# Deltanet and soft-MoE on one core: POOL's two-input work moved to VectorE and ScalarE, one form of inverse for all groups, a new order of work

## The chip, the cores and the metric

One core of a Trainium2 chip. The time is device microseconds of one execution, median of several runs. Engines: PE (TensorE), DVE (VectorE), ACT (ScalarE), POOL (GpSimd), SP (SyncE, here only a DMA queue).

## What is computed

A delta-rule attention scan over 768 steps for 4 batches x 8 heads of dimension 48, then a soft mixture of experts over its output. All is float32.

```python
k_n = k / (norm(k) + 1e-6)
for t in range(S):                       # S = 768
    y[t] = q[t] @ state
    v_old = state.T @ k_n[t]
    state += beta[t] * outer(k_n[t], v[t] - v_old)
x = y.transpose(...).reshape(3072, 384)
logits = x @ phi                         # 32 slots
d = softmax(logits, axis=0); slot_input = d.T @ x
slot_out[e] = relu(slot_input[e] @ w1[e]) @ w2[e]     # 8 experts, F = 1024
out = softmax(logits, axis=1) @ slot_out
```

## The kernel before, in words

The scan is cut into 24 chunks of 32 steps, and four chunks make a group (6 groups). For a chunk, all 32 (batch, head) pairs are worked on together.

*Preparation of a chunk* (`prep`, lines 472 to 561). K and Q are loaded padded (line 457), transposed by PE (543) and copied from PSUM (327 on ACT or 329 on DVE, a helper `copy`). PE forms the products K K^T and Q K^T (495). From them come L, in two masked ACT copies (507) whose halves are added (523, POOL or DVE), and A, copied in two halves and then masked on POOL (533, "mkA").

*Inverse of a group* (`invert`, 577 to 795). A DVE transpose brings the 32x32 matrices of 4 chunks x 32 pairs to one per partition (584, "spread"). Norms of k come from its diagonal (594 to 619; Newton steps on DVE for group 0, on POOL for the others). Then a forward elimination of 31 columns, each a product (648) and a subtraction (659) on DVE, each waiting for the one before. Line 663 transposes back, and `pairs` (566) writes two masked halves TP per chunk, on ACT (572) or POOL (574). Group 0 has another form: two 16-column eliminations side by side (704, 720), whose corner comes from small PE products (772, 785) and masks on POOL or ACT (758, 760).

*Scan of a chunk* (`chunk`, 802 to 889). V is scaled by the norms on POOL (813). PE reads the state (824), DVE subtracts (834), PE solves with TP (843), the result is copied, PE updates the state (860), whose four PSUM banks are copied in two parts of 64x768. A gives the output (876). Four DMAs a chunk re-lay it for the next stage (887, on SP's or ACT's queue).

*Routing of a group* (`route`, 895): transposes (903), logits (915), running column softmax, slot sums (971), row softmax (1000). *Experts*: weights are loaded by 56 DMAs (1026, 1034, on SP's queue) into the memory of scan buffers as these die; two layers (1119, 1150); outputs (1179, 1186 on ACT, 1188 on DVE) through 6 buffers, stored from SP and POOL (1192).

*The order.* Every operation is declared with the engines that could run it and a cost. `Plan.run` then simulates the engines ahead of the build: at each step it takes, for each engine, the ready operation of highest priority (length of the path behind it, plus a bias) among those that can start within 0.15 us of the first, and picks the engine whose choice starts first. The program is emitted in that order; on the chip each engine and queue works through its own list in order, waiting on semaphores.

Of the kernel before, what the change touches and what calls it, by code (L numbers as in the profile page):

```python
# [15 lines left out]
LAT = {"PE": 0.22, "DVE": 0.10, "ACT": 0.12, "POOL": 0.15, "SP": 0.05, "DMA": 1.9}  # L16
# [19 lines left out]
class Plan:  # L36
    def __init__(self, slots, banks, fixed, window):
        self.ops, self.slots, self.banks, self.window = [], slots, banks, window
        self.fixed, self.order, self.bias, self.limits = fixed, {}, 0.0, {}

# [3 lines left out]
    def op(self, name, engines, fn, reads=(), writes=(), bias=0.0, dma=0.0,  # L44
           uses=(), after=()):
        o = Op(name, engines, fn, list(reads), list(writes), bias + self.bias, dma)
# [57 lines left out]
    def run(self, backing=()):  # L104
# [23 lines left out]
        ready = [o for o in self.ops if not wait[o]]  # L128
# [21 lines left out]
        def place(v):  # L150
            if v.kind != "ps":
                if v.tag not in slots:
                    return 0.0, ()
                if self.order[v.tag][heads[v.tag]] is not v or not tags[v.tag]:
                    return None
                s = min(tags[v.tag])
                return s[0], s
            best = None
            n = v.banks
            if used.get(v.tag, 0) + n > self.limits.get(v.tag, 99):  # L160
                return None
            for i in range(0, self.banks - n + 1 if n < 4 else 1):
                if not any(held[i:i + n]):
                    t = max(bank[i:i + n])
                    if best is None or (t, -i) < (best[0], -best[1]):
                        best = (t, i)
            return best

        while left:
            pick = None  # L170
            for e in free:
                cands = []
                for o in ready:
                    for x, cost in o.engines:
                        if x != e:
                            continue
                        t = max([free[e]] + [seen(d, e) for d in o.deps])
                        ok = True
                        for v in o.writes:
                            if v.where is None:  # L180
                                p = place(v)
                                if p is None:
                                    ok = False
                                    break
                                t = max(t, p[0])
                            else:
                                t = max(t, v.avail)
                        if ok:
                            cands.append((t, o, cost))
                if not cands:  # L190
                    continue
                t0 = min(c[0] for c in cands)
                t, o, cost = max((c for c in cands if c[0] <= t0 + self.window),
                                 key=lambda c: (c[1].prio, -c[0]))
# [4 lines left out]
            for v in o.writes:  # L199
                if v.where is None:  # L200
                    p = place(v)
# [32 lines left out]
            for x in o.outs:  # L234
                wait[x] -= 1
                if not wait[x]:
                    ready.append(x)
# [6 lines left out]
def kernel(  # L244
# [11 lines left out]
    nc = tc.nc  # L256
# [9 lines left out]
    HC = C // 2  # L266
# [10 lines left out]
                lb=1056, tt=C * C, pr=256, Dt=512, Dc=512, M1=512, D0=1024,  # L277
                P1=512, TP=U * 2 * C, R=U * D, U=U * D, Y=U * D, S=4 * B * G * D, X=B * Dm,
                XT=B * P, lT=P, dT=P, d=P, el=P, cT=P, wt=NKT * F, hr=F, hT=NFC * P, ob=Dm,
                sj=Dm, so=Dm, cw=P, sl=NKT * NSL)  # L280
    SLOTS = dict(K=11, Q=4, V=5, KQ=10, AT=10, Lc=2, Lx=2, lb=2, tt=2, pr=2, Dt=1, Dc=1,
                 M1=1, D0=1, P1=1, TP=8, R=2, U=2, Y=3, S=2, X=2, XT=3, lT=2, dT=1, d=1, el=1,
                 cT=NG, hr=1, hT=2, ob=6, sj=1, so=1, cw=2, sl=1)
    ALIAS = {("X", 1): [("D0", 0), ("Dt", 0)], ("XT", 0): [("Dc", 0)], ("XT", 1): [("M1", 0)],
             ("XT", 2): [("P1", 0)]}
    KEEP = ("cT",)
    OBP, HTP, RBIAS, EB, IBIAS, FETCH = 0, 11, 40.0, 60.0, -5.0, 0.0125
    TAIL = ("hr", "hT", "ob", "sj", "so", "cw", "sl")
    plan = Plan(SLOTS, 8, 0, 0.15)
    plan.limits = dict(tp=2, pg=2, py=2)  # L290
# [49 lines left out]
    def vc(n):  # L340
        return 0.06 + 0.00104 * n
# [9 lines left out]
    half = const("half", [P, 2])  # L351
    par = const("par", [P, 2])
    tri2 = const("tri2", [P, 2, C])
# [36 lines left out]
    def constants2(e):  # L390
        nc.vector.tensor_tensor(bdm, bdm, hm.unsqueeze(2).broadcast_to([P, 4, C]), op=ALU.mult)
        nc.vector.tensor_reduce(tri, bdm.rearrange("p h t -> p t h"), axis=AX.X, op=ALU.add)
        nc.vector.tensor_reduce(half, ident.rearrange("p (h a t) -> p a h t", h=4, a=2),
                                axis=AX.XY, op=ALU.add)
        nc.vector.tensor_reduce(par, ident.rearrange("p (h a t) -> p a h t", h=2, a=2),
                                axis=AX.XY, op=ALU.add)
        nc.vector.tensor_tensor(tri2, tri.unsqueeze(1).broadcast_to([P, 2, C]),
                                par.unsqueeze(2).broadcast_to([P, 2, C]), op=ALU.mult)
    op("const2", [("DVE", 1.4)], constants2, [cv], [cv])

    padv, s0v, d0v = {}, [val("", "st") for _ in range(SLOTS["S"])], val("", "st")
# [11 lines left out]
    for i in range(SLOTS["S"]):  # L413
        op(f"s0{i}", [("POOL", 1.5), ("DVE", 1.5)], lambda e, i=i: clear(e, where["S", i]), [],
           [s0v[i]])
    op("d0", [("POOL", 0.6)],
       lambda e: clear(e, where["D0", 0].rearrange("p (u s) -> p u s", s=C)[:, :, HC:C]), [], [d0v])

# [22 lines left out]
    op("bbx", [("PE", 0.7)], spread_b, [btv, selv], [pbb])  # L441
# [20 lines left out]
    def loads(cc):  # L462
        for src, d, t in ((k, Kv, "K"), (q, Qv, "Q"), (v, Vv, "V")):
            x = d[cc] = val(t, par=True)
            for h in range(4):
                op(f"ld{t}{cc}", [("SP", 0.45)] + ([("ACT", 0.42)] if cc < 4 else []),
# [5 lines left out]
    def prep(cc):  # L472
# [37 lines left out]
        def ev_a(x, np_):  # L510
            def fn(e):
                for g in range(G):
                    copy(e, sb(at, G, B, 2, C)[:, g], view(x, np_, np_ - 1)[:, g])
            return fn

        def evs_l(x, np_):
# [8 lines left out]
            op(f"adL{cc}", [("POOL", 0.62), ("DVE", 0.35)], add, [lx, lcp[cc]], [lc, lcp[cc]])  # L525

        def evs_a(x, np_):
            op(f"evA{cc}", pcost2(512), ev_a(x, np_), [x], [at], bias=EB)

            def mask(e):  # L530
                v_ = nc.vector if e == "DVE" else PO
                t = sb(at, U, 2, C)
                v_.tensor_tensor(t, t, tri2.unsqueeze(1).broadcast_to([P, U, 2, C]), op=ALU.mult)  # L533
            op(f"mkA{cc}", [("POOL", 1.15)], mask, [at, cv], [at])

        for a, src, L in ((0, Kv, "K"), (1, Qv, "Q")):
            s = src[cc]
# [6 lines left out]
            op(f"tr{L}{cc}", [("PE", 0.46)], tr,  # L544
# [5 lines left out]
            if split:  # L550
                x = val("pg", "ps", 2)
                op(f"gram{L}{cc}", pe(16, 0.45), gram((a,), x), [kq], [x] + ([at] if a else [lc, lx]))
# [4 lines left out]
        if not split:  # L557
            x = val("pg", "ps", 2)
            op(f"gram{cc}", pe(16, 0.87), gram((0, 1), x), [kq], [x, lc, lx, at])
            evs_l(x, 2)  # L560
            evs_a(x, 2)


    TPv, nTv, TTp = {}, {}, {}

    def pairs(n, c, src, reads, uses):
        x = TPv[GC * n + c] = val("TP", par=True)
        for i in range(2):
            def fn(e, i=i):
# [3 lines left out]
                else:  # L573
                    PO.tensor_scalar(dst, src(), par[:, i:i + 1], None, op0=ALU.mult)
            op(f"TP{GC * n + c}", [("ACT", 0.42), ("POOL", 0.9)], fn, reads + [cv], [x], uses=uses)

    def invert(n):
        lc = Lcv[n]
        lb, tt = val("lb", par=n == 0), val("tt")
# [6 lines left out]
        op(f"spread{n}", [("DVE", 1.6)], spread, [lc], [lb])  # L586
# [14 lines left out]
        def newton(e):  # L601
            v_ = nc.vector if e == "DVE" else PO
            for _ in range(3):
                v_.tensor_tensor(gm, nr, dg(), op=ALU.mult)
# [5 lines left out]
        op(f"nw{n}", [(E0, 2.6 if n == 0 else 4.5)], newton, [lb, s1], [s1])  # L610
# [5 lines left out]
        op(f"gm{n}", [("DVE", 0.5)], inv, [s1, bbv], [gv])  # L616
# [5 lines left out]
        if n:  # L622
            lm = lambda: sb(lb)[:, 0:C * C].rearrange("p (i j) -> p i j", j=C)

            def zero(e):
                PO.memset(sb(tt), 0.0)
            op(f"ttz{n}", [("POOL", 1.0)], zero, [], [tt])

            def diag(e):
                PO.tensor_copy(sb(tt)[:, 0:C * C:C + 1], gm)  # L630
            op(f"ttd{n}", [("POOL", 0.4)], diag, [gv], [tt])

            def scale(e):
                (nc.vector if e == "DVE" else PO).tensor_tensor(
                    lm(), lm(),
                    gm.unsqueeze(2).broadcast_to([P, C, C]), op=ALU.mult)
            op(f"lbs{n}", [("DVE", 1.15), ("POOL", 1.95)], scale, [lb, gv], [lb])
            for j in range(C - 1):
                m, w = j + 1, C - 1 - j
                pr = val("pr")  # L640

                def e1(e, j=j, m=m, w=w, pr=pr):
                    t, s, o = sb(tt, C, C), lm(), sb(pr)[:, 0:w * m]
                    if m == 1:
                        nc.vector.tensor_tensor(o, t[:, 0, 0:1].broadcast_to([P, w]), s[:, 1:C, 0],
                                                op=ALU.mult)
                    else:
                        nc.vector.tensor_tensor(  # L648
                            o.rearrange("p (i k) -> p i k", i=w),
                            t[:, j, 0:m].unsqueeze(1).broadcast_to([P, w, m]),  # L650
                            s[:, j + 1:C, j].unsqueeze(2).broadcast_to([P, w, m]), op=ALU.mult)
                op(f"el{n}.{j}a", [("DVE", vc(w * m))], e1, [tt, lb], [pr])

                def e2(e, j=j, m=m, w=w, pr=pr):
                    t, o = sb(tt, C, C), sb(pr)[:, 0:w * m]
                    d = t[:, 1:C, 0] if m == 1 else t[:, j + 1:C, 0:m]
                    if m > 1:
                        o = o.rearrange("p (i k) -> p i k", i=w)
# [638 lines left out]
```

## Time and profile before

| | us |
|---|---|
| median of 3 runs (lowest, highest) | 410.18 (409.32, 416.75) |
| profiled execution | 405.77 |
| its span in the profile | 404.1 |
| DVE copies, line 329: 512 / 768 / 384 / 256 elements | 0.686 x31 / 0.955 x21 / 0.554 x20 / 0.415 x10 |
| ACT copies, line 327, same sizes | 0.598 x39 / 0.806 x25 / 0.492 x28 / 0.389 x38 |
| POOL lines 533 / 813 / 523 / 574, mean | 1.335 x24 / 0.875 x24 / 0.751 x21 / 1.183 x9 |
| line 584 transpose / 663 transpose / 634 scaling | 1.965 / 1.245 / 1.224 |
| weight loads, 512 and 384 KB, issue to landing | 6.6 and 6.2 |

Rows of the profile read "line engine operation, output<-input, shape, count | busy us in total, mean ns of one | idle time before, and who ended it". In a timeline a row gives start, duration, engine, line, and in brackets the idle time before it with its releaser. SPq and ACTq are DMA issues on those queues. Issues don't count as an engine's busy time, but take time in its order.

### The profile page before, as it was taken

What the parts mean: (1) busy time and instruction counts of PE and PEld (TensorE: products, weight loads), DVE (VectorE), ACT (ScalarE), POOL (GpSimd) and SP (SyncE); (2) the same over time, 40 slices, a digit from 0 to 9 for tenths busy, and PEclk for the clock granted to TensorE, in tenths of its full rate; (3) what the DMA queues carried; (4) which work ended last, traced back from release to release, by engine and by line L of the source; (5) the groups of instructions that cost most, each with busy time, mean ns of one, the idle gap of its engine ahead of it and who ended that gap; (6) DMA issues with size and microseconds to landing.
All of it is one profiled execution on the core that took longest, in us unless ns stands there. A gap on an engine that the chain in (4) does not pass through costs nothing. (4 is left out here: it accounts for less than half of the span.)

```text
span 404.1 us, 14058 instructions
## 1 busy us (share of the span) xinstructions
PE 280.0 (69%) x5940; PEld 216.9 (54%) x5940; DVE 277.7 (69%) x633; ACT 131.7 (33%) x277; POOL 119.5 (30%) x198
## 2 busy tenths in 40 slices
PE   4775747879467875787648686567769663679872
PEld 3664537768346763676547465455657452333330
DVE  5179877958759899799899769787995531332143
ACT  0552353314442423445244053162237110100032
POOL 7166436313551134645064004350012000000033
PEclk9687575869869988699957579958998968669985
DMA  7646450345414454243211325743319977798057
GB/s 131 109 88 103 84 91 13 58 75 87 80 27 81 71 89 70 36 77 57 41 19 24 68 54 140 259 135 80 59 29 360 367 247 210 243 384 319 1 210 259
DMA packets 115151, 49.84 MB, mean 123 GB/s; under 512 B 105760, under 2 KB 107296, under 8 KB 115088
## 3 DMA queue, kind: packets, MB, share of 16 engines
q1 hardware_dynamic: 90352, 42.20, 40.2%
q10 hardware_dynamic: 23936, 4.33, 6.0%
q0 software_dynamic: 800, 2.41, 1.7%
q8 instruction: 47, 0.77, 0.8%
q14 instruction: 16, 0.13, 0.1%
HBM read 39.47 MB, written 4.72 MB: 109 GB/s over the span
## 5 line engine op out<-in xcount | busy, mean ns | idle before, releaser
L327 ACT ACTIVATE arena<-banks 128x512 f32<-128x512 f32 (+4 forms) x139 | 71.1, 536 | 149.4 <-PE banks L876 36.3
L329 DVE COPY arena<-banks 128x512 f32<-128x512 f32 (+4 forms) x89 | 57.6, 658 | 58.5 <-PE banks L903 18.5
L659 DVE TENSOR_TENSOR arena<-arena 128x31 f32<-128x31 f32 (+15 forms) x155 | 61.7, 398 | 4.1
L648 DVE TENSOR_TENSOR arena<-arena 128x60 f32<-128x60 f32 (+9 forms) x150 | 61.5, 410 | 4.3
L824 PE MATMUL banks<-arena 128*32 128x96 f32 x1472 | 45.2, 271 | 10.3 <-ACT arena L327 4.9
L843 PE MATMUL banks<-arena 64*64 64x48 f32 x768 | 32.8, 244 | 22.8 <-DVE arena L834 15.0
L495 PE MATMUL banks<-arena 64*64 64x128 f32 (+1 forms) x896 | 35.3, 304 | 15.2 <-ACT arena L327 6.4
L843 PEld LDWEIGHTS banks<-arena 64*64 64x64 f32 x768 | 29.9, 159 | 27.7 <-DVE arena L834 14.6
L824 PEld LDWEIGHTS banks<-arena 128*32 128x32 f32 x1472 | 34.7, 120 | 17.9 <-ACT arena L327 10.5
L543 PE MATMUL banks<-ident,arena 128*128 128x128 f32 x192 | 34.1, 328 | 12.2 <-DMA arena<-in_k_dram 10.6
L523 POOL TENSOR_TENSOR arena<-arena 128x256 f32<-128x256 f32 x21 | 15.8, 751 | 81.1 <-ACT arena L507 62.7
L495 PEld LDWEIGHTS banks<-arena 64*64 64x64 f32 x896 | 28.4, 164 | 20.6 <-ACT arena L327 9.2
L507 ACT ACTIVATE arena<-banks,par 128x256 f32<-128x256 f32 x48 | 20.3, 471 | 46.6 <-PE banks L495 37.7
L543 PEld LDWEIGHTS banks<-ident,arena 128*128 128x128 f32 x192 | 25.8, 168 | 16.5 <-issue 6.3
L860 PE MATMUL banks<-arena 32*128 32x96 f32 x736 | 30.7, 311 | 5.2 <-DVE arena L329 3.4
L903 PE MATMUL banks<-ident,arena 128*128 128x128 f32 x72 | 16.0, 394 | 26.4 <-DMA arena<-arena 23.6
L813 POOL TENSOR_TENSOR arena<-arena,nTall 128x384 f32<-128x384 f32 x24 | 20.6, 875 | 45.6 <-DVE nTall L619 43.3
L533 POOL TENSOR_TENSOR arena<-arena,tri 128x512 f32<-128x512 f32 x24 | 31.9, 1335 | 5.8 <-DVE arena L329 5.0
L1192 POOL DMA_DIRECT2D out_dram<-arena x12 | 6.6, 551 | 88.5 <-DVE arena L1188 88.5
L860 PEld LDWEIGHTS banks<-arena 32*128 32x128 f32 x736 | 26.7, 216 | 9.8 <-DVE arena L329 4.6
L876 PE MATMUL banks<-arena 64*64 64x48 f32 x768 | 29.7, 229 | 1.4 <-issue 1.4
L572 ACT ACTIVATE arena<-arena,par 128x256 f32<-128x256 f32 x39 | 25.0, 709 | 16.4 <-DVE arena L663 8.2
(132 smaller groups left out, 317.1 us busy)
## 6 DMA issues: line engine op xcount, KB each, us to landing
arena<-in_moe_w_dram SPq DMA_DIRECT2D x24, 512.0 KB, 6.6
arena<-in_moe_w_dram SPq DMA_DIRECT2D x32, 384.0 KB, 6.2
arena<-in_q_dram SPq DMA_DIRECT2D x89, 48.0 KB, 2.4
arena<-in_k_dram SPq DMA_DIRECT2D x87, 48.0 KB, 2.3
arena<-in_v_dram SPq DMA_DIRECT2D x80, 48.0 KB, 2.4
arena<-arena ACTq DMA_DIRECT2D x56, 48.0 KB, 2.8
out_dram<-arena SPq DMA_DIRECT2D x12, 192.0 KB, 2.7
out_dram<-arena POOLq DMA_DIRECT2D x12, 192.0 KB, 2.8
```

What stands on the lines that cost most here:

```text
L327: AC.activation(dst, src, ACT.Copy)
L329: nc.vector.tensor_copy(dst, src)
L495: PE.matmul(t[hp_[hp], g, b * m:(b + 1) * m], lhsT=kt[rs_[g], b, 0, h2].rearrange("p h t -> p (h t)"), rhs=rhs, start=True, stop=True, ski ...
L533: v_.tensor_tensor(t, t, tri2.unsqueeze(1).broadcast_to([P, U, 2, C]), op=ALU.mult)
L543: PE.transpose(t[:, b, :], m[:, b, :], ident)
L572: AC.activation(dst, src(), ACT.Copy, scale=par[:, i:i + 1])
L648: nc.vector.tensor_tensor(o.rearrange("p (i k) -> p i k", i=w), t[:, j, 0:m].unsqueeze(1).broadcast_to([P, w, m]), s[:, j + 1:C, j].unsque ...
L659: nc.vector.tensor_tensor(d, d, o, op=ALU.subtract)
L824: PE.matmul(t[hs[h], b], lhsT=m[:, b, a, hs[h]], rhs=s[:, h, b], start=(b == 0), stop=False, skip_group_check=True)
L843: PE.matmul(t[hp_[i], b, g], lhsT=m[hp_[i], g, b], rhs=r[hp_[i], b, g], start=(b == 0 and g == 0), stop=True, skip_group_check=True)
L860: PE.matmul(banks[:, h, b * G * D:(b + 1) * G * D], lhsT=m[hs[h], b], rhs=r[hs[h], b], start=(cc == 0 and b == 0), stop=True, skip_group_c ...
L876: PE.matmul(t[hp_[i], b, g], lhsT=m[hp_[i], g, b], rhs=r[hp_[i], b, g], start=(cc == 0 and b == 0 and g == 0), stop=True, skip_group_check ...
```

## The change

- POOL no longer masks A: one DVE instruction reads PSUM, multiplies by the mask and writes A (`tri2` grows to hold it for four batches).
- The sum of L's halves (`adL`) is on DVE alone. V's scaling is on ACT, as eight activations of 48 columns with a scale per partition, or DVE. TP is on ACT or DVE. `lbs` is on DVE.
- Group 0 takes the 32-column inverse of the others; the 16-column form with its buffers, masks and products is deleted. Newton on DVE has three instructions a step for four.
- Weight loads are issued by POOL, re-layouts by SP alone, V loads by SP alone. There are 14 output buffers for 6.
- The planner: other costs and latencies (each cost lessened by LEAD), DVE taken for an operation that ACT could run too only if ACT would end over 2 us later (`shy`), another choice of PSUM banks, and a bias for each class of operation, from a table `TUNE` of some 300 numbers.

```diff
-LAT = {"PE": 0.22, "DVE": 0.10, "ACT": 0.12, "POOL": 0.15, "SP": 0.05, "DMA": 1.9}
+LAT = {"PE": 0.13, "DVE": 0.12, "ACT": 0.15, "POOL": 0.15, "SP": 0.05, "DMA": 2.0}
+LEAD = {"DVE": 0.08, "ACT": 0.1}
+TUNE = {
+    "AU.0": 376.3, "AU.1": -8.7, "AU.2": -16.9, "AU.3": -64.7, "AU.4": -50.7, "AU.5": 43.7,
...
+        engines = [(e, max(0.05, c - LEAD.get(e, 0.0))) for e, c in engines]
+        o = Op(name, engines, fn, list(reads), list(writes), 
+               bias + self.bias + TUNE.get(tune_key(name), 0.0), dma)
...
+                    for e, cost in o.engines:
+                        t = max(free[e], o.seen[e], w)
+                        if len(o.engines) > 1 and e in self.shy and min(
+                                free[x] + c for x, c in o.engines if x != e) - t - cost <= self.shy[e]:
                             continue
...
-                for g in range(G):
-                    copy(e, sb(at, G, B, 2, C)[:, g], view(x, np_, np_ - 1)[:, g])
+                nc.vector.tensor_tensor(
+                    sb(at, G, 2 * B, C),
+                    ps(x)[:, :, 0:B * np_ * 2 * C].rearrange(
+                        "p g (u a t) -> p g u a t", u=2 * B, a=np_)[:, :, :, np_ - 1],
+                    tri2.rearrange("p b h t -> p (b h) t").unsqueeze(1).broadcast_to(
+                        [P, G, 2 * B, C]), op=ALU.mult)
...
-            op(f"adL{cc}", [("POOL", 0.62), ("DVE", 0.35)], add, [lx, lcp[cc]], [lc, lcp[cc]])
+            op(f"adL{cc}", [("DVE", 0.38)], add, [lx, lcp[cc]], [lc, lcp[cc]])
...
-            op(f"mkA{cc}", [("POOL", 1.15)], mask, [at, cv], [at])
+            op(f"evA{cc}", [("DVE", 0.7)], ev_a(x, np_), [x, cv], [at], bias=EB)
...
+            plan.bias = (60.0, -60.0)[a] if split else 0.0
...
-                    PO.tensor_scalar(dst, src(), par[:, i:i + 1], None, op0=ALU.mult)
-            op(f"TP{GC * n + c}", [("ACT", 0.42), ("POOL", 0.9)], fn, reads + [cv], [x], uses=uses)
+                    nc.vector.tensor_scalar(dst, src(), par[:, i:i + 1], None, op0=ALU.mult)
+            op(f"TP{GC * n + c}", [("ACT", 0.7), ("DVE", 0.3)], fn, reads + [cv], [x], uses=uses)
...
-        if n:
...
-            op(f"lbs{n}", [("DVE", 1.15), ("POOL", 1.95)], scale, [lb, gv], [lb])
+        op(f"lbs{n}", [("DVE", 1.2)], scale, [lb, gv], [lb])
...
-            PO.tensor_tensor(t, t, f.unsqueeze(3).broadcast_to([P, B, G, D]), op=ALU.mult)
+            if e == "DVE":
+                nc.vector.tensor_tensor(t, t, f.unsqueeze(3).broadcast_to([P, B, G, D]), op=ALU.mult)
+                return
+            for b in range(B):
+                for g in range(G):
+                    AC.activation(t[:, b, g], t[:, b, g], ACT.Copy, scale=f[:, b, g:g + 1])
...
-        op(f"V{cc}", [("POOL", 0.86)], scale, [vv, nTv[n]], [vs])
+        op(f"V{cc}", [("ACT", 1.1), ("DVE", 0.56)], scale, [vv, nTv[n]], [vs])
...
-            op(f"rel{cc}", [("SP", 0.45), ("ACT", 0.41)], rel, [Yv], [X], dma=0.33,
+            op(f"rel{cc}", [("SP", 0.6)], rel, [Yv], [X], dma=0.33,
...
-            op(f"w1.{e}", [("SP", 0.45)], ld, [], [x], dma=1.35)
+            op(f"w1.{e}", [("POOL", 0.6)], ld, [], [x], dma=1.35)
...
-            op(f"w2.{e}", [("SP", 0.45)], ld, [], [x], dma=1.0)
+            op(f"w2.{e}", [("POOL", 0.6)], ld, [], [x], dma=1.0)
```

## The prediction

> **What bounds the kernel now.** I read the busy shares first, then busy time stage by stage, then the timeline of one stage, then the rows of the operations that move.
>
> ```profile
> PE 280.0 (69%) x5940; PEld 216.9 (54%) x5940; DVE 277.7 (69%) x633; ACT 131.7 (33%) x277; POOL 119.5 (30%) x198
> ```
>
> Two engines tie over the whole span, so the share decides nothing. I cut the span where an inverse ends (line 663, the transpose back, starts at 108.5, 159.3, 208.1, 261.7 and 299.8 us) and asked for busy time in those stretches. Columns: stretch, length, busy us (instructions) of PE, PEld, DVE, ACT, POOL, then granted clock, DMA share, GB/s.
>
> ```profile
> 24.80:52.20 27.40, 17.17 (x256) 13.83 (x247) 24.61 (x55) 9.88 (x26) 16.42 (x18) 0.75 0.56 96
> 52.20:108.50 56.30, 41.23 (x1308) 36.45 (x1308) 43.95 (x103) 23.70 (x53) 21.32 (x40) 0.78 0.38 65
> 108.50:159.30 50.80, 35.34 (x797) 29.92 (x801) 40.91 (x87) 17.75 (x34) 16.70 (x28) 0.84 0.40 69
> 159.30:208.10 48.80, 34.59 (x874) 29.38 (x867) 43.21 (x93) 20.12 (x41) 21.60 (x34) 0.88 0.30 52
> 208.10:261.70 53.60, 38.01 (x807) 29.98 (x799) 44.05 (x97) 18.21 (x41) 16.53 (x29) 0.79 0.40 102
> 261.70:301.00 39.30, 26.85 (x654) 22.04 (x654) 34.17 (x83) 14.27 (x26) 5.66 (x6) 0.83 0.33 77
> 301.00:338.00 37.00, 26.60 (x658) 22.06 (x658) 18.24 (x48) 10.98 (x24) 4.39 (x5) 0.86 0.84 279
> 338.00:404.00 66.00, 43.81 (x353) 19.50 (x353) 18.84 (x42) 9.59 (x20) 6.59 (x12) 0.77 0.67 242
> ```
>
> From 24.8 to 301 one inverse follows another, and DVE is 78 to 90% busy, the rest being mostly the 35 ns between dependent instructions. A middle period lasts 51.1 us on average, of which DVE works 42.7, PE 36.0, ACT 18.7. **DVE sets the period**; what it is relieved of comes off, until PE or ACT is next. After 301 it is another regime (last scan, DMA, experts).
>
> DVE's own work is slowed. In the timeline, four equal steps of the elimination:
>
> ```profile
> 140.24 0.43 DVE L659 TENSOR_TENSOR arena<-arena 128x255 f32<-128x255 f32 x1
> 140.70 0.83 DVE L648 TENSOR_TENSOR arena<-arena 128x252 f32<-128x252 f32 x1
> 141.57 1.38 DVE L659 TENSOR_TENSOR arena<-arena 128x252 f32<-128x252 f32 x1
> 142.98 0.42 DVE L648 TENSOR_TENSOR arena<-arena 128x247 f32<-128x247 f32 x1
> ```
>
> and POOL at that time:
>
> ```profile
> 140.29 0.96 POOL L523 TENSOR_TENSOR arena<-arena 128x256 f32<-128x256 f32 x1 [17.40 <-PE banks L876]
> 141.22 1.45 POOL L533 TENSOR_TENSOR arena<-arena,tri 128x512 f32<-128x512 f32 x1
> ```
>
> A DVE instruction with two SBUF inputs ends only when POOL's does: 0.42 us becomes 0.83 and 1.38. Instructions of these lines without POOL beside them follow 0.158 us + 1.04 ns per element. Comparing every DVE instruction with the median of its shape free of such overlap, the excess over the run is 27.9 us: 17.1 beside line 533, 5.3 beside 813, the rest beside 523 or two of them. By stretch: 7.5 in 24.8 to 52.2, 3.6 in the next, 5.3 on average in the middle periods, 2.0 and 1.5 in the two after. Instructions reading PSUM (lines 329, 834) show none.
>
> **The change, part by part.** Rows used:
>
> ```profile
> L834 DVE TENSOR_TENSOR arena<-arena,banks 128x384 f32<-128x384 f32 x23 | 12.7, 551 | 3.2 <-issue 2.0 <-DMA arena<-arena 0.4 <-PE banks L824 0.3
> L329 DVE COPY arena<-banks 64x768 f32<-64x768 f32 x21 | 20.1, 955 | 8.0 <-PE banks L860 6.7 <-ACT arena L327 0.8 <-PE banks L824 0.2
> L507 ACT ACTIVATE arena<-banks,par 128x256 f32<-128x256 f32 x48 | 20.3, 471 | 46.6 <-PE banks L495 37.7 <-DVE arena L704 4.3 <-PE banks L824 2.5
> L572 ACT ACTIVATE arena<-arena,par 128x256 f32<-128x256 f32 x39 | 25.0, 709 | 16.4 <-DVE arena L663 8.2 <-DVE arena L648 3.3 <-DVE arena L791 3.2
> ```
>
> *Middle period.* POOL loses lines 523, 533, 813 and 574; Newton, clears and diagonal stay. Contention: -5.3. Here a rule bears against me. The Trainium skill, "SBUF — State Buffer", section "Who interferes with whom", says that a DVE instruction with two SBUF inputs contends with any GpSimd instruction that reads SBUF, first come holding the port pair throughout. The trace agrees for the long two-input ones, but beside Newton's 128x32 instructions (0.27 us) and line 574 the mean excess is 0 to 0.13 us. By the rule the 5 x (13 x 0.27 + 0.8) = 22 us left on POOL could still block 3 to 4 us per period; by the rows 0.1. I take the rows.
> Added to DVE: line 523's sum, 4 x 0.42 (its three DVE runs) = 1.7; the masked eviction of A, one instruction of 512 from PSUM, 0.551 + 128 x 1.04 ns = 0.69, four = 2.8.
> Copies: the new rule lets DVE take a shared operation only where ACT would be over 2 us later. DVE has 8.6 us of copies per period. What remains, with V and TP falling to DVE, I call c: bounds 0 and 14.2 (all copies, four V at 0.56, eight TP at no more than 0.42, the full-rate price of 256 elements). I take 2.4, near the lower end, because ACT has room: 18.7, minus 2.5 for A's copies (38 x 0.389 / 6), plus 6.2 copies at 806/955 = 5.2, plus V. V is eight 128x48 activations: 512 to 128 elements runs 598 to 276 ns, so 48 are about 0.21, plus 0.08 for a scale pointer (471 against 389), less 0.1 overlap as line 507's pairs show: 0.2 each, 1.6 per V, 6.4 per period (the planner books 1.1). ACT: 28 of 44. Moreover 56 re-layout DMAs at 0.62 us leave ACT's queue, 5.8 per period.
> Sum: -5.3 + 1.7 + 2.8 - 8.6 + 2.4 = **-7.0**, so 44. Three periods -21; the last has less to lose (2.0 and part of 3.7 of copies): -4. Together **-25**.
>
> *Start to 108.5.* Group 0 gets the full inverse. Elimination: 62 x 0.158 + 10,912 elements x 1.04 ns = 21.1, with gaps 23.6; transposes 1.97 and 1.25, scaling 1.22, root, shorter Newton and reciprocal 3.5: 32.5 us after its spread at 24.8. Beside it DVE has eight A (5.5), two to four sums (1.3) and some 2 us of copies, so the factor stands near 66, the first solve (64.4 now) near 67, and group 1's spread moves from 52.2 to about 64. Group 1 then loses contention 3.6, the half-inverse's remains 3.7 and copies 5.8, gains 4.5 and some 4 of the idle 12.3 spent waiting for small products: 56.3 - 12.6 = 43.7. It ends at 107.7: **-1**; bounds -8 (K first in the load order) and +8 (no idle recovered). If that idle doesn't come back, the later spread shows. PE is rid of group 0's 512 small products (7.6 us, lines 772 and 785), in time that it had.
>
> *Last scan and tail.* ACT waits in its own queue:
>
> ```profile
> 320.75 3.62 ACTq L887 DMA_DIRECT2D arena<-arena  x2
> 324.42 0.31 ACT L1000 ACTIVATE arena<-arena 128x128 f32<-128x128 f32 x1 [4.24 <-DMA arena<-arena]
> 325.56 0.56 DVE L834 TENSOR_TENSOR arena<-arena,banks 128x384 f32<-128x384 f32 x1
> 345.39 1.08 PE L903 MATMUL banks<-ident,arena 128*128 128x128 f32 x4 [7.88 <-DMA arena<-arena]
> ```
>
> Two issues hold ACT 3.6 us, then line 1000, row work behind it on DVE, and the next chunk's line 834. With these DMAs on SP alone ACT doesn't stall: -4.2, and -1.5 contention: **-6**. At 338 the last re-layouts sit on SP among weight loads and PE idles 7.9. Weights go to POOL's queue: 56 issues leave SP (22 us at 0.39), 56 x 0.6 = 34 come for the re-layouts. I take **-3** (bounds 0 and -6: the bytes compete either way), and -1 for more output buffers (line 1188 waits 5.4 us for stores, line 1186 4.7 at the same time; the stores' own rate stays). In the same page, section "SBUF: two separate sides", DMAs issued by GpSimd starve while DVE runs a two-port operation. The row: POOL's stores took 0.55 us to issue and landed in 2.8 us against 2.7 from SP, on DVE reading PSUM. By the rule, 56 loads could wait 0.3 us behind a new TP each, 17 us of POOL's time, hidden since POOL becomes idle over half the span; I charge 0. What waits behind a weight load on POOL is Newton of group 5 (near 252, as loads begin at 248): at most about 4 us, once, in the range.
>
> What the new biases and costs do to the order, no row shows: at worst they undo the overlap (rivals 3 and 4), at best they fill DVE's idle (rival 1); I add nothing for them. Root, Newton, lbs (on DVE already, 1.22 five times) and constants stay within 1 us.
>
> Sum: -1 - 25 - 6 - 4 = -36. The profiled run took 405.77 us (span 404.1), so 370; the runs' median is 410.18, 1.1% more, so **374 us**.
>
> **Rivals.**
> 1. *More than that.* The new order packs down to PE: 36 busy plus 4 gives 40 per period, 13.5 less, and K first saves 5: 356. For it: unused DVE time of 8.4 per period. Against: dependent gaps. Chance 0.15.
> 2. *PE or ACT becomes the bound.* The granted clock of 0.84 falls to the 0.66 that many slices show: PE needs 45 of every period, 48 with gaps; gain 3, not 7: 388. ACT's underbooked V does the same. 0.15.
> 3. *Slower: DVE doesn't get rid of its copies.* If ACT's V and TP sit before urgent copies, these fall to DVE. Each us of c costs 4.6 over the run; at c = 10.2 nothing is gained, from 12.0 on it is 2% slower, at 14.2 it is 428. Against: ACT at 28 of 44. 0.12.
> 4. *It doesn't do what it says*: stalls end, but an in-order queue (SP's re-layouts behind loads that wait for buffers, POOL's Newton behind weights) takes the time back: 408. 0.08.
>
> **The numbers.** Forecast 0.50 (362 to 388). Faster by over 2% (what this measurement tells from no change): forecast, 1 and 2: 0.80; same 0.08; slower 0.12. The range 348 to 404 leaves out rival 3, most of 4 and little below.
>
> **What would show it.** Right: line 648's 128x252 near 0.42 in every run, periods near 44 between line 663's successors, DVE copies of 64x768 few, ACT busy near 190, first solve near 67, no ACT wait for a re-layout. Wrong: a period that stays at 50 with DVE below 80% busy, DVE copies unchanged, PE waiting for line 813's activations, or Newton waiting behind weight loads.

## The result and the profile after

The changed kernel takes **364.43 us** (median of 4 runs, 360.48 to 365.45); the kernel before took 411.31 beside it (409.32 to 416.75). The ratio is 0.886, 95% interval 0.876 to 0.895. The profiled execution took 364.28 us (span 362.6). In some executions, of any of these kernels, the chip grants a lower clock and the time is some per cent longer; ratios and intervals leave these out, medians don't.

First the busy shares of the changed kernel.

```profile
PE 262.5 (72%) x5428; PEld 200.9 (55%) x5428; DVE 215.9 (60%) x598; ACT 214.0 (59%) x523; POOL 70.7 (20%) x171
```

DVE lost 62 us, POOL 49, PE 17.5; ACT gained 82. For POOL, unlike the other engines, the profile counts DMA issues as busy: 36.6 of its 70.7 us, 6.6 of the 119.5 before. Its other work fell from 113 to 34 us. Inverses now end (line 770, the transpose back, starts) at 60.9 for group 0, then 104.3, 147.7, 191.4, 235.5 and 265.1. Busy time in those stretches, changed kernel, columns as in the prediction (the cut at 293.5 is 2.3 us before the last output copy ends, where the table below cuts):

```profile
18.50:60.90 42.40, 21.45 (x388) 17.64 (x387) 35.54 (x97) 21.71 (x62) 4.19 (x12) 0.83 0.59 97
60.90:104.30 43.40, 32.03 (x692) 28.17 (x692) 32.57 (x86) 27.82 (x67) 5.85 (x19) 0.73 0.33 57
104.30:147.60 43.30, 35.45 (x846) 29.38 (x847) 35.20 (x93) 30.98 (x78) 6.72 (x17) 0.88 0.43 73
147.60:191.40 43.80, 33.33 (x777) 27.70 (x779) 32.03 (x90) 31.22 (x79) 5.05 (x16) 0.88 0.43 72
191.40:235.50 44.10, 36.35 (x881) 30.48 (x871) 32.86 (x89) 32.20 (x80) 9.96 (x25) 0.88 0.49 123
235.50:266.40 30.90, 22.27 (x674) 19.17 (x671) 26.85 (x72) 23.07 (x60) 0.80 (x2) 1.00 0.41 92
266.40:293.50 27.10, 22.73 (x597) 18.69 (x597) 6.39 (x22) 16.61 (x33) 5.66 (x11) 0.94 0.78 261
293.50:362.60 69.10, 49.49 (x452) 22.23 (x444) 7.24 (x26) 22.95 (x53) 25.19 (x47) 0.79 0.76 279
```

A middle period is 43.7 us, and now **no** engine is near it: PE 35, DVE 33, ACT 31. The difference between the two spans, by stage:

| stage | before | after | measured | predicted |
|---|---|---|---|---|
| start to group 1's inverse end | 108.5 | 104.3 | -4.2 | -1 |
| from there to group 5's, four periods | 191.3 | 160.8 | -30.5 | -25 |
| last scan, to its last output copy | 38.3 | 30.7 | -7.6 | -6 |
| the rest | 66.0 | 66.8 | +0.8 | -4 |
| sum | 404.1 | 362.6 | -41.5 | -36 |

The groups of the changed kernel that answer to the moved work, different shapes kept apart:

```profile
L607 DVE TENSOR_TENSOR arena<-banks,tri 128x512 f32<-128x512 f32 x24 | 16.3, 683 | 4.8 <-ACT arena L602 4.8
L622 DVE TENSOR_TENSOR arena<-arena 128x256 f32<-128x256 f32 x24 | 10.0, 425 | 18.7 <-ACT arena L602 18.7
L797 ACT ACTIVATE arena<-arena,nTall 128x48 f32<-128x48 f32 x192 | 45.6, 323 | 9.0 <-DMA arena<-in_v_dram 8.9
L818 DVE TENSOR_TENSOR arena<-arena,banks 128x384 f32<-128x384 f32 x23 | 12.7, 553 | 35.5 <-PE banks L808 20.9 <-ACT arena L427 11.0 <-DMA arena<-arena 3.3
L753 DVE TENSOR_TENSOR arena<-arena 128x252 f32<-128x252 f32 x12 | 5.0, 419 | 0.3
```

A's masked eviction (683 ns) and the sum (425) cost what I had charged. V went to ACT whole, eight activations in 1.9 us, for my 1.6. The long elimination steps run at 0.42 us: the excess of all the elimination's instructions over 0.158 us + 1.04 ns per element fell from 25.5 to 0.4 us. The subtraction (818, before 834) now idles 35.5 us where it idled 3.2: DVE waits for PE's and ACT's scan work. And of DVE's shared copies, in the kernel before one of its three largest groups, none is left:

```profile
L329 DVE COPY arena<-banks 128x512 f32<-128x512 f32 (+4 forms) x89 | 57.6, 658 | 58.5 <-PE banks L903 18.5 <-PE banks L543 11.7 <-PE banks L1138 7.4
```

I had read only the first number of this row's busy part, by shape. The second part, **58.5 us of idle time in front of these copies**, is as large, and I had left it out. Of it 37.4 us lie after 301, in the last scan and the tail; in the three middle periods it is 17.7 us.

### The profile page after: what moved, and what is told of

It reads as the page before. It is cut to its first block, busy times and chain, and to the rows that moved or that the text cites. A ratio compares the mean times of both kernels' runs of the same rounds, so it can differ in the third digit from the quotient of the medians.

```text
span 362.6 us, 13124 instructions
## 1 busy us (share of the span) xinstructions
PE 262.5 (72%) x5428; PEld 200.9 (55%) x5428; DVE 215.9 (60%) x598; ACT 214.0 (59%) x523; POOL 70.7 (20%) x171
## 4 chain that ended last, share of the span: by engine, by line
PE 31%; DMA 17%; ACT 17%; SPq 10%; DVE 10%; issue 10%; POOL 2%; ACTq 0%; POOLq 0%; DVEq 0%
SPq L552 9%; ACT arena L427 8%; PE banks L808 7%; DMA arena<-arena 7%; PE banks L827 5%; ACT arena L797 5%; DMA arena<-in_v_dram 4%; PE banks L590 4%; PE banks L844 3%; PE banks L860 3%; DMA arena<-in_k_dram 3%; DVE arena L766 2%; DVE arena L753 2%; PE banks L637 2%; DMA arena<-in_moe_w_dram 2%
## 5 line engine op out<-in xcount | busy, mean ns | idle before, releaser
L427 ACT ACTIVATE arena<-banks 128x512 f32<-128x512 f32 (+3 forms) x176 | 102.2, 599 | 76.6 <-PE banks L637 17.8
L637 PE MATMUL banks<-ident,arena 128*128 128x128 f32 x192 | 34.1, 316 | 26.5 <-DMA arena<-in_k_dram 11.8
L797 ACT ACTIVATE arena<-arena,nTall 128x48 f32<-128x48 f32 x192 | 45.6, 323 | 9.0 <-DMA arena<-in_v_dram 8.9
L827 PEld LDWEIGHTS banks<-arena 64*64 64x64 f32 x768 | 29.3, 155 | 23.1 <-ACT arena L667 13.5
L590 PEld LDWEIGHTS banks<-arena 64*64 64x64 f32 x896 | 30.1, 171 | 11.1 <-ACT arena L427 7.7
L818 DVE TENSOR_TENSOR arena<-arena,banks 128x384 f32<-128x384 f32 x23 | 12.7, 553 | 35.5 <-PE banks L808 20.9
L667 ACT ACTIVATE arena<-arena,par 128x256 f32<-128x256 f32 x46 | 31.0, 731 | 4.3 <-DVE arena L770 4.3
L860 PEld LDWEIGHTS banks<-arena 64*64 64x64 f32 x768 | 26.0, 142 | 6.5 <-issue 3.7
L1010 POOL DMA_DIRECT2D arena<-in_moe_w_dram x24 | 13.0, 543 | 84.0 <-issue 30.7
L704 POOL TENSOR_TENSOR gmall<-nrall,arena 128x32 f32<-128x32 f32 x15 | 4.6, 305 | 125.5 <-DVE nrall L691 124.7
L844 PEld LDWEIGHTS banks<-arena 32*128 32x128 f32 x736 | 24.5, 200 | 5.5 <-ACT arena L427 2.9
L622 DVE TENSOR_TENSOR arena<-arena 128x256 f32<-128x256 f32 x24 | 10.0, 425 | 18.7 <-ACT arena L602 18.7
```

The lines of the kernel that those rows point to most:

```text
L427: AC.activation(dst, src, ACT.Copy)
L590: PE.matmul(t[hp_[hp], g, b * m:(b + 1) * m], lhsT=kt[rs_[g], b, 0, h2].rearrange("p h t -> p (h t)"), rhs=rhs, start=True, stop=True, ski ...
L637: PE.transpose(t[:, b, :], m[:, b, :], ident)
L667: AC.activation(dst, src(), ACT.Copy, scale=par[:, i:i + 1])
L797: AC.activation(t[:, b, g], t[:, b, g], ACT.Copy, scale=f[:, b, g:g + 1])
L827: PE.matmul(t[hp_[i], b, g], lhsT=m[hp_[i], g, b], rhs=r[hp_[i], b, g], start=(b == 0 and g == 0), stop=True, skip_group_check=True)
```

## The experiments

What had to be told apart: my account (freed DVE time is the gain), an account by which the new order is the gain and the moves little, and what each part is worth alone. Ratios are to the kernel before, beside which each ran. Where it doesn't say "order kept", the planner made a new order for the run, so such a run tests its edit together with the order that follows from it.

### The parts alone

**No biases**: the changed kernel with an empty table.

```diff
-TUNE = {... some 300 numbers ...}
+TUNE = {}
```

> The changed kernel with the table of searched biases emptied; engines, costs and the rule that keeps DVE shy stay. Engine theory (the gain is DVE freed of stalls and of copies): the order only fills idle time, 364 to 376 us, DVE copies stay near zero. Order theory (the search makes most of the gain): 385 us or more, with periods between inverses near 50.

Measured: 392.66 us, ratio 0.959 (0.948 to 0.969). Inverses end at 56.0, 110.1, 149.8, 189.4, 227.5, 284.2. The three middle periods together and the last, in this run:

```profile
110.10:227.50 117.40, 91.56 (x2085) 76.40 (x2085) 92.78 (x247) 84.07 (x212) 12.69 (x36) 0.85 0.37 71
227.50:284.20 56.70, 43.98 (x1066) 36.76 (x1062) 36.78 (x102) 30.06 (x69) 12.49 (x30) 0.83 0.71 189
```

The biases are worth 28 us, but not where I looked: the middle is *faster* without them (117.4 us for 131.2). They gain 5.8 us at the start, 27.1 in the last inverse and 7.0 after it, which looks like work put off in the middle that piles up at the end. The spread of group 0 begins at 25.4 in it, as before the change (24.8), and not at 18.5: the early start is the biases' work. As everything but the biases is in this run, the prediction's assumption that biases add nothing was wrong by as much as 28 us.

**The moves alone**: the kernel before with A's mask in the eviction, the sum on DVE, V and TP off POOL, `lbs` on DVE; its own planner and form of inverse kept.

```diff
-            op(f"mkA{cc}", [("POOL", 1.15)], mask, [at, cv], [at])
+            op(f"evA{cc}", [("DVE", 0.7)], ev_a(x, np_), [x, cv], [at], bias=EB)
...
-        op(f"V{cc}", [("POOL", 0.86)], scale, [vv, nTv[n]], [vs])
+        op(f"V{cc}", [("ACT", 1.1), ("DVE", 0.56)], scale, [vv, nTv[n]], [vs])
```

> The kernel before with only the POOL work moved (mask of A fused into its eviction on DVE, sum and scaling on DVE, V and TP on ACT or DVE), its own planner, group 0's half inverse and queues kept. My sum per period: stalls -5.3, added 4.5, some V and TP +2, copies unchanged: about +1, so 405 to 418 us: the moves alone bring nothing, since the work goes where the time is short. Rival (the stalls are what matters): about 28 us less, 380 to 388.

Measured: 418.71, ratio 1.022 (1.009 to 1.034). The elimination's excess fell to 0.7 us and DVE's busy time stayed, 281 us for 278. Taking the stalls away by these moves **costs** 7 us under the old planner, a little more than I expected at most. The middle periods stay at 51.0 us with 42.0 of DVE's work (51.1 and 42.7 before), so there -5.3 and +4.5 nearly cancelled, as the sum says; most of the loss lies ahead of them, where group 1's inverse ends at 116.6 for 108.5.

**The moves undone** in the changed kernel, with its planner and biases.

```diff
-            op(f"evA{cc}", [("DVE", 0.7)], ev_a(x, np_), [x, cv], [at], bias=EB)
+            op(f"evA{cc}", pcost2(512), ev_a(x, np_), [x], [at], bias=EB)
+            op(f"mkA{cc}", [("POOL", 1.3)], mask, [at, cv], [at])
...
-        op(f"V{cc}", [("ACT", 1.1), ("DVE", 0.56)], scale, [vv, nTv[n]], [vs])
+        op(f"V{cc}", [("POOL", 0.86)], scale, [vv, nTv[n]], [vs])
```

> The changed kernel with POOL's two-input work back (mask of A, sum, V, TP), new planner, biases and sharing rule kept. My sum per period against the changed kernel: stalls +5.3, DVE work -4.5: about +1, so 365 to 375 us, if ACT's relief from V doesn't count. Rival (the stalls are what matters): 385 us or more. Third (ACT is the next bound, V off it helps): 355 to 362.

Measured: 406.33, ratio 0.993 (0.988 to 0.999). The inverses end at 66.4, 107.7, 151.3, 183.3, then 268.2 and 270.5: two run side by side. The planner made another order, with biases searched for another set of operations, so this run doesn't isolate the moves; what makes it slow stays open. DVE carries none of the shared copies in it either, so their absence alone doesn't make a kernel fast. The two runs that follow keep the order instead.

**The inverse of group 0 alone**, in the kernel before.

```diff
-        lb, tt = val("lb", par=n == 0), val("tt")
+        lb, tt = val("lb"), val("tt")
...
-        if n:
+        if True:
```

> The kernel before with the 32-column inverse for group 0 too, nothing else. My step: first solve some 3 us later, next inverse begins up to 12 later, part given back: 412 to 424 us. Rival (group 0's form makes no difference, since the start waits for loads and products): 408 to 412.

Measured: 437.91, ratio 1.069 (1.058 to 1.080), more than I expected: inverses end at 123.7 (15 us later) and at 329.9. The last period ran at a granted clock of 0.50, and the four runs at 0.74 to 0.77 (0.78 to 0.83 for the kernel before beside them), so part of the loss may be the clock. Alone, under the old planner, the new form costs 26 us; at the start of the changed kernel (-4.2) nothing of it is to be seen.

### Is DVE's busy time the period?

**The mask back on POOL, order kept**: in the changed kernel DVE copies A plainly (as long as before) and POOL masks it in place.

```diff
-                nc.vector.tensor_tensor(sb(at, G, 2 * B, C), ps(x)..., tri2..., op=ALU.mult)
+                nc.vector.tensor_copy(t, ps(x)...)
+                PO.tensor_tensor(t, t, tri2..., op=ALU.mult)
```

> The changed kernel, order kept: DVE evicts A with a plain copy of the same length and POOL masks it in place, as before. DVE theory (the period is DVE's work): 24 stalls of about 0.7 us each in the elimination, 374 to 384 us. Rival (DVE now has some 10 us of idle time a period that takes them up): 363 to 369 us, with the stalls visible in the durations of the elimination's instructions.

Measured: 364.53, ratio 0.898 (0.892 to 0.904; its companion runs of before had a median of 408.27): **hardly changed**, though the stalls are back. The time is the changed kernel's, measured on another chip; by the ratios (0.898 for 0.886, the intervals just touch) some 5 us of the stalls may show. Groups of this run:

```profile
L754 DVE TENSOR_TENSOR arena<-arena 128x60 f32<-128x60 f32 (+9 forms) x180 | 74.3, 413 | 5.3
L767 DVE TENSOR_TENSOR arena<-arena 128x31 f32<-128x31 f32 (+15 forms) x186 | 69.3, 373 | 5.5
L623 DVE TENSOR_TENSOR arena<-arena 128x256 f32<-128x256 f32 x24 | 10.9, 465 | 15.0 <-ACT arena L602 15.0
```

and the same of the changed kernel (its sum was shown above, with 18.7 us of idle before it):

```profile
L766 DVE TENSOR_TENSOR arena<-arena 128x31 f32<-128x31 f32 (+15 forms) x186 | 63.7, 342 | 5.5
L753 DVE TENSOR_TENSOR arena<-arena 128x60 f32<-128x60 f32 (+9 forms) x180 | 62.5, 347 | 5.3
```

The elimination takes 17.4 us more, DVE's busy time is 20 us more (235.8), and the waits shrink: in a middle period DVE works 36.3 us for 33.4, and its waits over 0.1 us are 3.1 us for 8.3. (These periods were 41.5 us for 43.7, at a granted clock of 0.93 for 0.88; the stretches before and after them took longer.) DVE, in order, comes later to instructions that had waited for others anyhow.

**The same test on the kernel before**: order kept, POOL's mask of A and its scaling of V replaced by one-input multiplications by 1. This leaves out A's mask and the norms in V.

```diff
-                v_.tensor_tensor(t, t, tri2..., op=ALU.mult)
+                v_.tensor_scalar(sb(at), sb(at), 1.0, None, op0=ALU.mult)
...
-            PO.tensor_tensor(t, t, f..., op=ALU.mult)
+            PO.tensor_scalar(sb(vv), sb(vv), 1.0, None, op0=ALU.mult)
```

> The kernel before, order kept, with POOL's mask of A and scaling of V replaced by one-input instructions on the same data (a multiplication by one): the causal mask of A and the norms in V are left out. This takes most of the 27.9 us of stalls from DVE and changes nothing else. DVE theory (before, DVE set the period): 384 to 392 us. Rival (as in the changed kernel, where stalls put back cost nothing): 402 to 411 us.

Measured: 408.81 (407.98, 411.29, 409.64, 401.64), beside 411.56. Three of the four, the profiled one too, ran at a granted clock of 0.77 to 0.78, so no interval is given, and the gain is put at no more than the 10 us of the lowest, at 0.79. Groups of this run:

```profile
L329 DVE COPY arena<-banks 128x512 f32<-128x512 f32 (+4 forms) x89 | 57.7, 659 | 69.5 <-PE banks L902 18.1 <-PE banks L542 17.3 <-PE banks L859 8.9
...
L833 DVE TENSOR_TENSOR arena<-arena,banks 128x384 f32<-128x384 f32 x23 | 12.7, 552 | 12.2 <-PE banks L823 4.9 <-POOL arena L812 3.4 <-issue 2.7
```

DVE is relieved of 18 us (277.7 to 259.6). Idle time in front of the copies rises from 58.5 to 69.5, in front of the subtraction from 3.2 to 12.2: 20 us in all. Part of this may be the clock: 0.78 in the middle periods for 0.83 before, PE busy 294 us for 280. My account asked for 384 to 392, or 393 for the 18 us that really went. It is **contradicted**, as at most 10 of the 18 us came off; that all of them turned into waiting isn't shown.

**One-input work on POOL**, beside the changed kernel's own: 24 multiplications by 1 on A's buffer, order kept.

```diff
                         [P, G, 2 * B, C]), op=ALU.mult)
+                PO.tensor_scalar(sb(at), sb(at), 1.0, None, op0=ALU.mult)
```

> The changed kernel, order kept, with an added POOL instruction after each eviction of A that multiplies it in place by one (128x512, one SBUF input). If any POOL instruction that reads SBUF blocks DVE instructions with two SBUF inputs: their durations show 24 stalls and the time is that of the run with the mask on POOL. If one-input instructions don't block, as the rows of before suggest: no stall over 0.1 us on average, and 363 to 367 us.

Measured: 364.15, ratio 0.886 (0.881 to 0.890), unchanged. What it shows of the hardware is told at the end.

### Whose work sits in DVE's list

**Only the sharing rule**: the kernel before, with three lines in the planner's loop: DVE takes a shared operation only where the other engine, ACT or POOL, would end over 2 us later. Nothing else of the change; the order is planned anew.

```diff
+                        if ok and e == "DVE" and len(o.engines) > 1 and min(
+                                free[x] + c for x, c in o.engines if x != e) - t - cost <= 2.0:
+                            ok = False
```

> The kernel before with one thing added to its planner: DVE takes an operation that another engine can run too only if the other would be over 2 us later. Copies leave DVE for ACT (8.6 us a period), POOL's work and its stalls stay. DVE theory at 4.6 us per us: 375 to 390 us. Rival (the order around it decides, each alone brings little): 400 us or more.

Measured: **373.01**, ratio 0.905 (0.898 to 0.911): 38 of the 47 us. Inverses end at 106.8, 153.1, 194.9, 237.0, 272.7; the middle stretches of this run, and its largest DVE groups:

```profile
106.80:153.10 46.30, 36.23 (x859) 31.04 (x857) 33.10 (x76) 27.20 (x53) 20.37 (x32) 0.88 0.42 72
153.10:194.90 41.80, 35.33 (x845) 30.07 (x845) 37.99 (x78) 24.95 (x50) 24.69 (x40) 0.89 0.40 67
194.90:237.00 42.10, 35.73 (x862) 29.42 (x862) 38.11 (x87) 25.35 (x56) 20.80 (x27) 0.88 0.41 92
```

```profile
L662 DVE TENSOR_TENSOR arena<-arena 128x31 f32<-128x31 f32 (+15 forms) x155 | 68.8, 444 | 4.9
L651 DVE TENSOR_TENSOR arena<-arena 128x60 f32<-128x60 f32 (+9 forms) x150 | 64.8, 432 | 4.5
L837 DVE TENSOR_TENSOR arena<-arena,banks 128x384 f32<-128x384 f32 x23 | 12.7, 551 | 19.3 <-PE banks L827 12.5 <-DMA arena<-arena 5.2 <-DMA arena<-in_k_dram 0.8
```

The elimination is slower than ever (133.6 us against 123.2 before: more stalls, excess 37.2), and still the mean middle period is 43.4 us, the changed kernel's. DVE's copies are gone but for one, and the five scalings `lbs` (1.22 us each) went to POOL.

**The other way round**: the changed kernel, order kept, its 46 copies of 64x768 (the state) on DVE for ACT.

```diff
-            o.fn(o.eng)
+            o.fn("DVE" if o.name.startswith("evS") else o.eng)
```

> The changed kernel, order kept, with all 46 state copies of 64x768 moved from ACT to DVE: 44 us more on DVE (c up by 7.3 a period), 37 us less on ACT. My figure of 4.6 us per us of c: 395 to 400 us. Rival (ACT, PE and the chain between them are now as long as DVE's work): 366 to 378 us.

Measured: 380.42, ratio 0.935 (0.930 to 0.940), 16 us slower (20 by the ratios). Their group in this run:

```profile
L429 DVE COPY arena<-banks 64x768 f32<-64x768 f32 x46 | 43.9, 953 | 19.5 <-PE banks L844 18.8
```

The 43.9 us bring 19.5 us of waiting for PE with them. The state copies, moved back with the order kept, cost 16 to 20 us, not the 34 that my rate of 4.6 us a microsecond of c gave; the other waits absorb the rest.

**V on DVE**, order kept.

```diff
-            o.fn(o.eng)
+            o.fn("DVE" if o.name[0] == "V" else o.eng)
```

> The changed kernel, order kept, with the scaling of V moved from ACT (eight activations, 1.9 us) to DVE (one instruction, some 0.55 us): DVE 2.2 us a period more, ACT 7.6 less. DVE theory at 4.6 us per us: 374 us. Rival (ACT holds the chain now): 350 to 362 us. If both have slack: 362 to 366.

Measured: 361.34, ratio 0.886 (0.880 to 0.892). One DVE instruction of 554 ns takes the place of eight activations; ACT is rid of 41 us, DVE has 9 more, and the time falls by 3, near the spread of the runs; the ratio is the changed kernel's. So ACT's busy time isn't the bound either.

### The end

**Weights on SP**, order kept.

```diff
-            o.fn(o.eng)
+            o.fn("SP" if o.name[:3] in ("w1.", "w2.") else o.eng)
```

> The changed kernel, order kept, with the 56 weight loads issued from SP's queue again. My step (weights off SP gain 3 us or more at the last re-layouts): 367 to 375 us. Rival (no gain, since the same bytes compete for the same engines): 363 to 366 us. Third (POOL's descriptors are the slower way): below 362.

Measured: 364.76, ratio 0.884 (0.878 to 0.890): the queue of the weights makes no difference to the time.

**A candidate**: V on DVE, every second output on DVE, half of the last re-layouts on ACT's queue.

```diff
+            if o.name[:3] == "evo" and int(o.name[-1]) % 2:
+                o.eng = "DVE"
+            if o.name[0] == "V":
+                o.eng = "DVE"
+            if o.name in ("rel22", "rel23"):
+                last += 1
+                o.eng = ("SP", "ACT")[last % 2]
```

> A candidate on the changed kernel, order kept: V on DVE (one instruction for eight activations), every second output scaled on DVE, and the last two chunks' re-layouts issued half from SP and half from ACT. From the run with V on DVE: 361, less 1 to 3 at the outputs and 1 at the re-layouts: 356 to 360 us. Rival (the outputs wait for their stores anyway, the re-layouts for their bytes): 360 to 362.

Measured: 361.53, ratio 0.874 (0.865 to 0.882), as with V alone. The interval overlaps the changed kernel's, so it isn't shown to be faster.

## Why the prediction was right, and where it wasn't

The time (364 for 374, inside 362 to 388) and the periods (43.7 for 44) were right. That they were is in part luck: the stalls were counted in full and the copies too low, which cancelled, and the biases, counted as nothing, made up for what other parts of the change lost.

*"DVE sets the period; what it is relieved of comes off."* **This step failed in part.** It rested on the reading that DVE's idle time is "mostly the 35 ns between dependent instructions", and that was wrong. Before, a middle period of DVE was 42.7 us of work, 2.0 of small gaps and 6.4 of waits over 0.1 us, of which 5.8 stood in front of copies. With the sharing rule alone it was 36.4, 2.2 and 4.8; after the whole change 33.4, 2.1 and 8.3. So the work fell by 9.3 us, just what the terms give with c at 0 (-5.3 + 1.7 + 2.8 - 8.6 = -9.4), but 2 of it came back as waits, and the period fell by 7.4. After the change DVE is far from setting the period. The page of the changed kernel follows the chain of work that ended last back through the whole span; by engine (SPq: issuing DMAs; issue: no wait that the profile shows):

```profile
PE 31%; DMA 17%; ACT 17%; SPq 10%; DVE 10%; issue 10%; POOL 2%; ACTq 0%; POOLq 0%; DVEq 0%
```

In the middle periods (104.3 to 235.5) this chain is PE 40%, ACT 29%, DMAs and their issue 24%, and DVE 2%. For the kernel before it can be followed only back to 332.7, so the trace doesn't tell what set the period there. My explanation, argued and not isolated: DVE carried two chains in one list, the elimination, each step waiting for the last, and the scan's copies, each waiting for a PE product that itself waits for copies. What the elimination saved was in part waited for at the next copy.

*Contention, -5.3 a period* (the stretches of the prediction add up to 30.5 us, not to its 27.9): worth at most some 5 of 20 us in the new order, and at most 10 of 18 us, by the lowest run, in the old one. The stalls were real (0.42 us became 1.38); they delayed work that in good part would have waited. *Moved work, +1.7 and +2.8*: sizes right; under the old planner the moves as a whole cost 7 us, outside the middle periods.

*Copies, -8.6 + 2.4 = -6.2*: mis-sized. c was about 0, and a copy that waits takes its wait too out of DVE's list: 8.6 + 5.8 = 14.4 us per period. The rule alone shortened the period by 7.7 us, 6.3 of it DVE's work and 1.6 its waits, while stalls rose and other waits came up (19.3 us over the run at the subtraction, 16.7 at the start of the inverses, there mostly for POOL). All else together moved it by +0.3. ACT, with every copy, was busy for 214 us, not near 190.

*Start, -1*: -4.2. The spread came at 18.5 for 24.8, the "K first" of my lower bound; from it to the end of group 0's transpose back 43.6 us for the 41 of the prediction (whose terms add up to 31.5, not 32.5, before the other work); the first solve at 63.5 for 67.

*Last scan, -6*: -7.6; ACT's wait for a re-layout is gone (4.24 us before line 1000, nothing before its successor, line 984). *The rest, -4*: +0.8, **missed**. PE still waits for the last re-layouts, issued one after another on SP. From the end of the last output copy to the first transpose behind these DMAs it is 7.0 us, and was 7.3:

```profile
292.99 5.44 SPq L871 DMA_DIRECT2D arena<-arena  x5
...
302.80 2.79 PE L887 MATMUL banks<-ident,arena 128*128 128x128 f32 x12 [2.57 <-DMA arena<-arena]
```

and moving the weights off SP brought nothing: the bound of 0 which I had named, with the reason that the bytes compete either way, which the runs don't show by itself. By the Trainium skill ("SBUF — State Buffer", section "SBUF: two separate sides"), a DMA issued by GpSimd waits for its descriptors while VectorE runs a two-port operation. It cost nothing here, where few of DVE's instructions can be of that kind (13 copies or `tensor_scalar` within SBUF, 2.9 us, while the weights load): 512 and 384 KB landed in 6.5 and 7.5 us from POOL, in 6.6 and 7.8 from SP in the run with the weights there, and the totals agree.

*Biases at nothing*: 28 us. From the sharing rule alone (373) to the whole change without biases (393) the other parts lose 20 us (17.6 between the profiled spans: +3.3 at the start, -12.8 in the middle periods, +21.0 in the last inverse, +6.1 after it); the biases win them back and 9 more. How this divides among group 0's inverse, the moves and the planner's other edits isn't settled: sharing rule, moves and old planner together weren't tried.

*Rivals.* PE, DVE or ACT as the new bound: DVE took 20 us more and ACT 41 us less for a change of 3 us or less, and PE has 35 of 43.7 and wasn't tried. What sets 43.7 us is, by the chain above, work that passes between PE, ACT and DMAs; in other runs that keep this order DVE's share of it is 9 to 39%, highest with V on DVE, so several chains are nearly as long. *The order, not the sharing of work*: not excluded. Runs with the sharing rule and new orders range from 364 to 406 us, and the rule alone came with a new order too; the state copies moved back with the order kept (16 to 20 us) are the direct test. *The clock*: in the middle periods 0.83 before and 0.88 with the rule alone and after the change; its part in the gain wasn't separated. "DVE doesn't get rid of its copies" did not occur, and its price of 4.6 us per us of c was too high: 16 to 20 us for 7.3 us a period is 2.2 to 2.7.

## What to carry to other kernels

Read both halves of a group's row: an instruction that waits for another engine costs an in-order engine its wait as well as its work, and time freed ahead of it on that engine can turn into more waiting. Cut the idle time by stage, as you do the work, and ask the chain of work that ended last whether the busiest engine is in it at all. Then take work that waits for other engines out of the list of the engine that runs a long dependent chain, before making that chain faster. When a change has several parts, run its cheapest rule alone: here three lines of the planner, with the order that came of them, brought 38 of 47 us, while the moves off POOL lost 7 by themselves.

## What the runs showed of the hardware

A POOL instruction with **one** input holds up DVE far less than one with two. In the run with multiplications by 1 (1.54 us each), 78 elimination instructions beside one took 77 ns more on average; beside a two-input mask (1.32 us), 37 of them took 508 ns more. The first elimination instruction to begin beside a multiplication by 1 took 0.29 to 0.46 us longer in 18 of 20 cases and always ended before POOL's; beside a mask it took 0.5 to 1.1 us longer and always ended after POOL's (19 cases). Timeline of the run with one-input work:

```profile
212.46 1.60 POOL L613 TENSOR_SCALAR arena<-arena 128x512 f32<-128x512 f32 x1 [7.79 <-DVE arena L607]
...
212.74 0.70 DVE L754 TENSOR_TENSOR arena<-arena 128x247 f32<-128x247 f32 x1
...
213.48 0.42 DVE L767 TENSOR_TENSOR arena<-arena 128x247 f32<-128x247 f32 x1
```

The Trainium skill ("SBUF — State Buffer", section "Who interferes with whom") lets a DVE instruction with two SBUF inputs contend with any GpSimd instruction that reads SBUF, and the later one wait until the first has ended. By this rule the 0.70, begun after POOL's, could not end before 214.06, where POOL's does. Here it ends at 213.44, and the next one runs its undisturbed 0.42 within POOL's time. For two-input instructions the rule and the trace agree: in the prediction's timeline the 1.38 ends at 142.95, POOL's mask at 142.67.
